# Convolution taps of chunk 0 as products with diagonal matrices, in a fused attention and gated feed-forward kernel

## The chip, the cores and the metric

The kernel runs on one core of one Trainium2 chip. That core has a matrix engine (TensorE, PE in the profile, its weight loads PEld), a vector engine (VectorE, DVE), an activation engine (ScalarE, ACT), a general engine (GpSimd, POOL) and a queue engine (SyncE, SP). The metric is the device time of one execution in microseconds, and lower is better.

## What is computed

```python
# attention, for batch 4, 8 heads, 768 rows, head size 64
k_sum = k.reshape(B, H, nb, 32, D).max(axis=3)      # one key per block of 32
v_sum = v.reshape(B, H, nb, 32, D).mean(axis=3)
scores_l = scale * q @ k.T      # kept where |row - column| < 16
scores_s = scale * q @ k_sum.T + log(32)
a = softmax(concat([masked scores_l, scores_s]))
x = a @ concat([v, v_sum])      # heads side by side: (4, 768, 512)
# feed-forward
h = maximum(x @ w_in, 0)        # (4, 768, 1024)
conv_out = sum over k in 0..2 of conv_w[k] * (h shifted by k - 1 rows)
gate = 1 / (1 + exp(-conv_out))
out = (h * gate) @ w_out
```

Everything is float32.

## The kernel before

A sequence of 768 rows is cut in two chunks of 384 rows, so four batches make eight chunks, numbered 0 to 7. Within a chunk attention runs over four pairs of heads. The feed-forward part is worked on transposed: the 1024 hidden features lie on partitions in eight blocks (`fc` 0 to 7), the rows along the free dimension. One block of one chunk is a unit.

The large products with `w_in` and `w_out` are done in three reduced-precision terms each: a number is split into a high and a low part (`win_hi`, `win_lo`, `xh`, `xl`, `ghi`, `glo`, `wout_hi`, `wout_lo`), and high by high, high by low and low by high are added up in PSUM. The weights come in as 64-bit words and are decoded and split on the core (`decode`, `weights`: lines 97 to 104 on ACT and DVE, 127 on ACT, 128 on POOL). Scores (line 260), weighted values (line 329) and transposes (line 308) are products of plain float32.

A unit goes like this. `f1` (line 404) does 12 matmuls of 384 or 386 columns into a PSUM tile with the tag `f1`, of which there are three buffers. `gate_conv` rectifies the tile in place on ACT (line 422), makes the middle tap of the convolution in a new SBUF tile `t` (line 425 on ACT for the chunks in `TAP_ACT`, line 427 on DVE for the others), and adds the outer two taps on DVE (line 434), reading the PSUM tile at shifted columns. `gate_mul` takes the tanh on ACT (line 451), multiplies on DVE with the rectified rows (line 452), rounds to `ghi` on ACT (line 455) and makes `glo` on POOL (line 456). `gate_mul` runs one unit later than `gate_conv`; the PSUM tile is free after line 452. `f2` (line 473) contracts the gated rows with `w_out`, in pieces spread over the units of the next chunks, and line 482 with a DMA on ACT's queue stores the result.

Chunk 0 starts with the attention of its own rows alone (the loop at line 507), while the inputs arrive in the order of `LOADS` on SP's queue. The convolution weights are the item `c` of that list (line 504), and are decoded after the loop (line 518). Units 0 and 1 of chunk 0 do three quarters of their first product early (line 521). The weights `w_out` are split from unit 6 of chunk 0 on (`OUT_AT`). `WARM` adds idle matmuls (line 78) in chunk 0, three behind each unit's first product.

The order of the instructions on each engine is made by a planner from the program's order and its own idea of their lengths. From chunk 2 on (`ORDERED`), the order of the matrix engine is that of the program. On each engine the instructions run in that fixed order, and a wait holds up what stands behind it.

Of the kernel before, what the change touches and what calls it, by code (L numbers as in the profile page):

```python
# [7 lines left out]
F32 = mybir.dt.float32  # L8
F32R = mybir.dt.float32r
U32 = mybir.dt.uint32  # L10
AF = mybir.ActivationFunctionType
ALU = mybir.AluOpType
# [3 lines left out]
DM, DF = 512, 1024  # L16
P = 128
# [9 lines left out]
CH = S // 2  # L27
CB = CH // QB
NCC = DM // P
NFC = DF // P  # L30
# [3 lines left out]
DEPTH = 2  # L34


TAP_ACT = (0, 1, 2, 4)


LOADS = "k0 q0 k1 q1 v0 k2 q2 a0 v1 k3 q3 a1 w0 v2 c a2 w1 v3 a3 w2 w3 w4 w5 w6 w7"  # L40
EARLY_IN = 2

OUT_AT = (6, 7, 8, 9, 10, 10, 11, 12)
# [7 lines left out]
def attention_ffn(ctx, tc, qT, kT, vT, v4, w_in, cwT, w_out, mask8, ident_in, out):  # L51
    nc = tc.nc
    cp = ctx.enter_context(tc.tile_pool(name="cp", bufs=1))
    sp = ctx.enter_context(tc.tile_pool(name="sp", bufs=2))
    ps = ctx.enter_context(tc.tile_pool(name="ps", bufs=1, space=bass.MemoryType.PSUM))
# [3 lines left out]
    ident = cp.tile([P, P], F32, name="ident")  # L59
    cw = cp.tile([P, NFC, 3], F32, name="cw")  # L60
    win_hi = cp.tile([P, NFC, NCC, P], F32R, name="win_hi")
    win_lo = cp.tile([P, NFC, NCC, P], F32R, name="win_lo")
    wout_hi = cp.tile([P, NFC, DM], F32R, name="wout_hi")
    wout_lo = cp.tile([P, NFC, DM], F32R, name="wout_lo")

    raw_a = cp.tile([P, 6, 1024], U32, name="raw_a", tag="big_a")
    raw_b = cp.tile([P, 6, 1024], U32, name="raw_b", tag="big_b")
# [21 lines left out]
    def decode(out, words, n, name):  # L89

        lo_word = words[:, 0 : 2 * n : 2]
        hi_word = words[:, 1 : 2 * n : 2]
        low = sp.tile([P, DM], U32, tag="wl", name=f"wl_{name}", bufs=1)[:, :n]
        nc.scalar.activation(
            out.bitcast(F32), hi_word.bitcast(F32), AF.Abs, scale=2.0**-112
        )
        nc.vector.tensor_scalar(low, lo_word, 29, None, ALU.logical_shift_right)  # L100
        nc.vector.scalar_tensor_tensor(
            out, out, 3, low, ALU.logical_shift_left, ALU.bitwise_or
        )
        nc.vector.scalar_tensor_tensor(
            out, hi_word, 0x80000000, out, ALU.bitwise_and, ALU.bitwise_or
        )
# [12 lines left out]
        return t  # L119

    def split_out(fc, t):
        weights(t, wout_hi[:, fc, :], wout_lo[:, fc, :], f"o{fc}")

    def weights(words, hi, lo, name):
        w = sp.tile([P, DM], U32, tag="wu", name=f"wu_{name}", bufs=3)
        decode(w, words, DM, name)
        nc.scalar.copy(hi, w.bitcast(F32))  # L127
        nc.gpsimd.tensor_tensor(lo, w.bitcast(F32), hi.bitcast(F32), ALU.subtract)  # L128
# [8 lines left out]
    for tag in ("xh", "xl"):  # L137
        t = sp.tile([P, 2, KL], F32, tag=tag, name=f"k_{tag}", bufs=2)
# [11 lines left out]
    def load_k(c, p):  # L150
        b, hf = divmod(c, 2)
        i = c * NP + p
        st = state[(c, p)] = {}
        if i == NP - 1:
            kw = sp.tile([P, 1024], F32, tag="stage", name=f"kw{i}", bufs=2)
            st["kw"] = kw[:, : CB * NK].rearrange("p (b k) -> p b k", b=CB)
        else:
            st["kw"] = sp.tile([P, CB, NK], F32, tag="kw", name=f"kw{i}", bufs=3)
        if hf == 0:
            if c == 0:  # L160
                k = spare[p]
            else:
                k = sp.tile([P, KL], F32, tag="kT", name=f"kT{i}", bufs=2)
            nc.sync.dma_start(k, kT[b, p, :, :KL])
            st["k"] = k
        if c:
            first = kT[b, p, :, hf * CH : hf * CH + WK]
            nc.sync.dma_start(st["kw"][:, :, :WK], window(first, 1, [SP, P], WK))

    def load_vt(c, p):  # L170
        b, hf = divmod(c, 2)
        i = c * NP + p
        if hf:
            return
        if b == 0:
            v = raw_b[:, 2 + p, :S].bitcast(F32)
        else:
            v = sp.tile([P, 1024], F32, tag="stage", name=f"vt{i}", bufs=2)[:, :S]
        nc.sync.dma_start(v, vT[b, p])
        state[(c, p)]["vt"] = v  # L180
# [15 lines left out]
    def load_vm(c, p):  # L196
        vm = state[("vm", c // 2, p)]
        nc.sync.dma_start(
            state[(c, p)]["va"][WK:NK, :, :], vm.unsqueeze(1).to_broadcast([NB, CB, P])
        )  # L200
# [158 lines left out]
    def slot(j):  # L359

        if j % 2 == 0:
            n = j // 2 + 2
            if NP <= n < npair:
                load_k(*divmod(n, NP))
                load_vt(*divmod(n, NP))
            if NP <= j // 2 < npair:
                load_vm(*divmod(j // 2, NP))
            if j // 2 < npair:
                qk(*divmod(j // 2, NP))
        else:  # L370
            n = (j + 1) // 2
            if NP <= n + 1 < npair:
                load_q(*divmod(n + 1, NP))
            if n < npair:
                c, p = divmod(n, NP)
                if c:
                    vmean_pair(c, p)
                    load_v(c, p)
                prep_pair(c, p)
# [32 lines left out]

    held = {}

    def gate_conv(c, fc):


        hf = c % 2
        n = CH + 2 * hf
        ng = CH - 1 + 2 * hf  # L420
        h = f1ps.pop((c, fc))
        nc.scalar.activation(h[:, :n], h[:, :n], AF.Relu)
        t = sp.tile([P, CH + 2], F32, tag="t", name=f"t{c}_{fc}", bufs=3)[:, :ng]
        if c in TAP_ACT:
            nc.scalar.activation(t, h[:, hf : hf + ng], AF.Copy, scale=cw[:, fc, 1:2])  # L425
        else:
            nc.vector.tensor_scalar(
                t, h[:, hf : hf + ng], cw[:, fc, 1:2], 1.0, ALU.mult, ALU.mult
            )
        for k in (0, 2):  # L430

            i0 = max(0, 1 - hf - k)
            i1 = min(ng, n - (hf + k - 1))
            nc.vector.scalar_tensor_tensor(  # L434
                t[:, i0:i1],
                h[:, hf + k - 1 + i0 : hf + k - 1 + i1],
                cw[:, fc, k : k + 1],
                t[:, i0:i1],
                ALU.mult,
                ALU.add,  # L440
            )
        held[(c, fc)] = h, t

    def gate_mul(c, fc):

        hf = c % 2
        ng = CH - 1 + 2 * hf
        d0 = (CH - 1) * hf
        h, t = held.pop((c, fc))
        hi = gated["hi"][:, fc, d0 : d0 + ng]  # L450
        nc.scalar.activation(t, t, AF.Tanh, scale=0.5)  # L451
        nc.vector.scalar_tensor_tensor(  # L452
            t, t, 1.0, h[:, hf : hf + ng], ALU.add, ALU.mult
        )
        nc.scalar.copy(hi, t)  # L455
        nc.gpsimd.tensor_tensor(  # L456
            gated["lo"][:, fc, d0 : d0 + ng], t, hi.bitcast(F32), ALU.subtract
        )
# [3 lines left out]
    def f2(b, st, fcs, tag="f2", bufs=1):  # L462
        if fcs[0] == 0:
            f2ps[(b, st)] = ps.tile([P, 512], F32, tag=tag, name=f"f2_{b}_{st}", bufs=bufs)
        po = f2ps[(b, st)]
        ss = slice(st * P, (st + 1) * P)
        ghi, glo = gated["hi"], gated["lo"]
        for fc in fcs:
            contracted.add((b, st, fc))
            for m, (gx, w) in enumerate(  # L470
                ((ghi, wout_hi), (ghi, wout_lo), (glo, wout_hi))
            ):
                nc.tensor.matmul(  # L473
                    po,
                    gx[:, fc, ss],
                    w[:, fc, :],
                    start=(fc == 0 and m == 0),
                    stop=(fc == NFC - 1 and m == 2),
                )
        if fcs[-1] == NFC - 1:  # L480
            ob = sp.tile([P, DM], F32, tag="wu", name=f"ob{b}_{st}", bufs=3)
            nc.scalar.activation(ob, po, AF.Copy, scale=0.5)  # L482
            nc.scalar.dma_start(out[b, ss, :], ob)
# [3 lines left out]
    cw_words = sp.tile([P, 2 * NFC * 3], U32, tag="cww", name="cw_words", bufs=1)  # L487
    nc.scalar.dma_start(mask, mask8)
    nc.scalar.dma_start(ident, ident_in)

    for item in LOADS.split():
        what, n = item[0], int(item[1:] or 0)
        if what == "k":
            load_k(0, n)
        elif what == "q":
            load_q(0, n)
        elif what == "v":
            load_vt(0, n)
        elif what == "a":
            load_v(0, n)  # L500
        elif what == "w":
            raws[n] = load_in(n)
        else:
            nc.sync.dma_start(cw_words, cwT.bitcast(U32))

    prep_pair(0, 0)
    for j in range(2 * NP):
        slot(j)
        if j % 2 == 0:
            vmean_pair(0, j // 2)  # L510
        slot_t(j)
        slot_av(j)
# [2 lines left out]
            slot_t(j)  # L515
        slot_av(j)

    decode(cw.rearrange("p f k -> p (f k)").bitcast(U32), cw_words, NFC * 3, "cw")
    for fc in range(EARLY_IN):
        split_in(fc, raws[fc])  # L520
    for cc in range(3):
# [158 lines left out]
```

## Time and profile before

| what | value |
|---|---|
| median of 3 timed runs | 409.43 us (408.94, 409.43, 410.58) |
| span of the profiled execution, first to last instruction | 408.4 us |
| instructions | 8852 |
| mean granted clock of the matrix engine | 0.986 |
| first and last rectification of a unit (line 422), start | 41.2 us, 380.1 us |
| first products of chunk 0's unit 2 begin | 59.09 us |

The profile has the span alone for its execution; the median stands 1.0 us above that span. Busy time counts an engine's running instructions, not its waits; matmuls overlap, so a busy matrix engine is not one at its peak. The granted clock is the share of full speed that the matrix engine's throttle let through. Where a timeline row ends in brackets, they hold the idle time before it and what ended it.

### The profile page before, as it was taken

How to read it: one execution, taken by the hardware profiler on the slowest of the kernel's cores; microseconds unless marked ns; L12 is line 12 of the kernel's file. 1: busy time of each engine (PE TensorE's matmuls, PEld its weight loads, DVE VectorE, ACT ScalarE, POOL GpSimd, SP SyncE). 2: the span in 40 equal slices, each digit the busy share in tenths (PEclk: the TensorE clock that was granted, in tenths of full speed). 3: DMA queues.
4: the chain of work that ended last, by engine and by line, in shares of the span. 5: the costliest groups of instructions: out<-in, count | busy, mean ns of one | idle time of the engine just before them, and what ended most of it. 6: DMA issues, size and time to landing. Idle time of an engine off the chain costs nothing.

```text
span 408.4 us, 8852 instructions
## 1 busy us (share of the span) xinstructions
PE 385.8 (94%) x3173; PEld 319.2 (78%) x3173; DVE 269.9 (66%) x809; ACT 251.8 (62%) x774; POOL 150.7 (37%) x179
## 2 busy tenths in 40 slices
PE   7989669997799999999999999999999999999996
PEld 3546458785678888888888888888788888898884
DVE  4999888999956765768775466556566665566200
ACT  3664887997867676757566777666564654343211
POOL 2226564477754233333333333333332232112100
PEclk9999989999969999999999999999999999999999
DMA  8999943767865784456344344344220000000011
GB/s 290 331 367 202 258 138 114 227 185 223 225 145 170 240 285 126 127 154 181 85 111 112 78 112 112 77 120 119 66 63 27 28 0 27 26 27 26 27 51 51
DMA packets 60715, 54.47 MB, mean 133 GB/s; under 512 B 24640, under 2 KB 51328, under 8 KB 60672
## 3 DMA queue, kind: packets, MB, share of 16 engines
q1 hardware_dynamic: 56928, 47.19, 41.4%
q10 hardware_dynamic: 3744, 6.73, 4.6%
q8 instruction: 25, 0.41, 0.4%
q14 instruction: 18, 0.15, 0.1%
HBM read 45.55 MB, written 6.29 MB: 127 GB/s over the span
## 4 chain that ended last, share of the span: by engine, by line
PE 62%; ACT 14%; DVE 13%; POOL 5%; issue 4%; DMA 1%; SPq 0%; ACTq 0%; POOLq 0%; DVEq 0%
PE f L473 26%; PE f L404 23%; ACT a L288 6%; PE pt L308 4%; PE xp L329 4%; PE pq L260 4%; DVE t L434 4%; ACT t L451 2%; PE pw L78 2%; POOL glo L456 2%; DVE t L452 1%; POOL a L300 1%; DMA k_xh<-kT 1%; ACT ghi L455 1%; POOL wout_lo L128 1%
## 5 line engine op out<-in xcount | busy, mean ns | idle before, releaser
L456 POOL TENSOR_TENSOR glo<-t,ghi 128x383 fp32r<-128x383 f32 (+1 forms) x64 | 66.8, 1044 | 128.5 <-ACT ghi L455 124.4
L404 PE MATMUL f<-xh,win_hi 128*128 128x384 f32 (+1 forms) x256 | 93.4, 365 | 0.9 <-ACT win_hi L127 0.9
L434 DVE SCALAR_TENSOR_TENSOR t<-f,cw,t 128x382 f32<-128x382 f32 (+3 forms) x128 | 78.7, 615 | 20.7 <-ACT t L425 17.8
L404 PE MATMUL f<-xl,win_hi 128*128 128x384 f32 (+1 forms) x256 | 87.8, 343 | 0.0
L404 PE MATMUL f<-xh,win_lo 128*128 128x384 f32 (+1 forms) x256 | 87.3, 341 | 0.0
L288 ACT ACTIVATE a<-a,nm 128x120 f32<-128x120 f32 x192 | 73.1, 382 | 9.9 <-DVE nm L278 9.7
L473 PE MATMUL f<-wout_lo,ghi 128*128 128x512 f32 x192 | 76.0, 396 | 2.4 <-POOL wout_lo L128 2.4
L473 PE MATMUL f<-wout_hi,ghi 128*128 128x512 f32 x192 | 76.2, 397 | 0.0
L473 PE MATMUL f<-wout_hi,glo 128*128 128x512 f32 x192 | 75.3, 393 | 0.0
L451 ACT ACTIVATE t<-t 128x383 f32<-128x383 f32 (+1 forms) x64 | 33.6, 525 | 63.8 <-DVE t L434 63.2
L300 POOL TENSOR_TENSOR a<-a,sm 128x360 f32<-128x360 f32 x56 | 45.4, 832 | 55.2 <-DVE sm L297 51.4
L452 DVE SCALAR_TENSOR_TENSOR t<-t,f 128x383 f32<-128x383 f32 (+1 forms) x64 | 35.3, 552 | 26.6 <-ACT t L451 26.6
L404 PEld LDWEIGHTS f<-xh,win_hi 128*128 128x128 f32 x256 | 49.1, 192 | 3.6 <-ACT win_hi L127 1.2
L404 PEld LDWEIGHTS f<-xl,win_hi 128*128 128x128 f32 x256 | 49.2, 192 | 0.7 <-issue 0.2
L404 PEld LDWEIGHTS f<-xh,win_lo 128*128 128x128 f32 x256 | 48.9, 191 | 0.2
L473 PEld LDWEIGHTS f<-wout_lo,ghi 128*128 128x128 f32 x192 | 36.2, 189 | 8.9 <-POOL wout_lo L128 3.0
L455 ACT CAST ghi<-t 128x383 fp32r<-128x383 f32 (+1 forms) x64 | 32.5, 508 | 16.4 <-DVE t L452 15.6
L278 DVE CUSTOM_DVE_ANT_0 a<-pq,mask 128x120 f32<-128x120 f32 x192 | 42.2, 275 | 0.0
L473 PEld LDWEIGHTS f<-wout_hi,glo 128*128 128x128 f32 x192 | 36.2, 188 | 7.7
L308 PE MATMUL pt<-ident,a 128*120 128x128 f32 x192 | 34.4, 285 | 7.8 <-ACT aT L315 3.6
L473 PEld LDWEIGHTS f<-wout_hi,ghi 128*128 128x128 f32 x192 | 36.3, 189 | 6.4 <-ACT ob L482 0.3
L260 PEld LDWEIGHTS pq<-kw,q 64*64 64x64 f32 x768 | 23.3, 133 | 20.8 <-issue 12.8
(59 smaller groups left out, 506.7 us busy)
## 6 DMA issues: line engine op xcount, KB each, us to landing
va<-v SPq DMA_DIRECT2D x32, 288.0 KB
kw<-kT SPq DMA_DIRECT2D x28, 288.0 KB
q<-qT SPq DMA_DIRECT2D x32, 192.0 KB
out_dram<-ob ACTq DMA_DIRECT2D x24, 256.0 KB
kT<-kT SPq DMA_DIRECT2D x12, 392.0 KB
vt<-vT SPq DMA_DIRECT2D x12, 384.0 KB
wo<-w_out SPq DMA_DIRECT2D x8, 512.0 KB
raw_a<-w_in SPq DMA_DIRECT2D x6, 512.0 KB
```

The lines of the kernel that those rows point to most:

```text
L260: last = nc.tensor.matmul(pq[h][half * QB : (half + 1) * QB, i * NK : (i + 1) * NK], st["q"][r, blk * QB : (blk + 1) * QB], st["kw"][r, bl ...
L278: nc.vector.tensor_tensor_reduce(a[:, i, :], pq[h][:, i * NK : (i + 1) * NK], mask[:, hf, i, :], -0.125, 3.0e38, ALU.add, ALU.min, nm[:, h ...
L288: nc.scalar.activation(a[:, i, :], a[:, i, :], AF.Exp, bias=nm[:, h, i : i + 1], scale=-1.0, accum_out=sm[:, h, i : i + 1],)
L300: (nc.gpsimd if n >= NP else nc.vector).tensor_tensor(a, a, sm[:, h, :].unsqueeze(2).to_broadcast([P, 3, NK]), ALU.mult)
L308: last = nc.tensor.transpose(pt[:NK, i * P : (i + 1) * P], a[:, i, :], ident)
L404: last = nc.tensor.matmul(ph[:, :n], w[:, fc, cc, :], x[:, cc, :n], start=(cc == 0 and m == 0), stop=(cc == NCC - 1 and m == 2),)
L434: nc.vector.scalar_tensor_tensor(t[:, i0:i1], h[:, hf + k - 1 + i0 : hf + k - 1 + i1], cw[:, fc, k : k + 1], t[:, i0:i1], ALU.mult, ALU.add,)
L451: nc.scalar.activation(t, t, AF.Tanh, scale=0.5)
L452: nc.vector.scalar_tensor_tensor(t, t, 1.0, h[:, hf : hf + ng], ALU.add, ALU.mult)
L455: nc.scalar.copy(hi, t)
L456: nc.gpsimd.tensor_tensor(gated["lo"][:, fc, d0 : d0 + ng], t, hi.bitcast(F32), ALU.subtract)
L473: nc.tensor.matmul(po, gx[:, fc, ss], w[:, fc, :], start=(fc == 0 and m == 0), stop=(fc == NFC - 1 and m == 2),)
```

## The change

For chunk 0 alone (`TAP_PE`), the three taps become three float32 products on the matrix engine. The stationary operand of tap `k` is a diagonal matrix that holds the 128 weights of the block; the moving operand are the rectified rows, shifted by `k - 1` columns, and the three add up in a PSUM tile of the tag `f1`. For that the rows are rectified out of PSUM into an SBUF tile (`rows`), the tanh works in place on the PSUM tile, and line 452's product goes from both to an SBUF tile `t`.

The diagonals (128 x 384 for the three taps of a block) are made by POOL in eight operations, one in each turn of the first attention loop, from the identity matrix and the decoded weights. So the convolution weights are loaded earlier, on ACT's queue, and decoded after the first turn. Rows and diagonals have the memory of `wout_hi` and `wout_lo`, which become one tile for each block. The list of chunks whose middle tap ACT makes goes from 0, 1, 2, 4 to 1, 2, 3, 5.

```diff
-TAP_ACT = (0, 1, 2, 4)
+TAP_ACT = (1, 2, 3, 5)
+TAP_PE = (0,)
-LOADS = "k0 q0 k1 q1 v0 k2 q2 a0 v1 k3 q3 a1 w0 v2 c a2 w1 v3 a3 w2 w3 w4 w5 w6 w7"
+LOADS = "k0 q0 k1 q1 v0 k2 q2 a0 v1 k3 q3 a1 w0 v2 a2 w1 v3 a3 w2 w3 w4 w5 w6 w7"
...
-    wout_hi = cp.tile([P, NFC, DM], F32R, name="wout_hi")
-    wout_lo = cp.tile([P, NFC, DM], F32R, name="wout_lo")
+    wout_hi, wout_lo = {}, {}
+    rows = [cp.tile([P, DM], F32, name=f"row{fc}", tag=f"wh{fc}") for fc in range(NFC)]
+    diag = [cp.tile([P, DM], F32, name=f"diag{fc}", tag=f"wl{fc}") for fc in range(NFC)]
...
     def split_out(fc, t):
-        weights(t, wout_hi[:, fc, :], wout_lo[:, fc, :], f"o{fc}")
+        wout_hi[fc] = cp.tile([P, DM], F32R, name=f"wout_hi{fc}", tag=f"wh{fc}")
+        wout_lo[fc] = cp.tile([P, DM], F32R, name=f"wout_lo{fc}", tag=f"wl{fc}")
+        weights(t, wout_hi[fc], wout_lo[fc], f"o{fc}")
...
+    def taps(fc):
+        return diag[fc][:, : 3 * P].rearrange("p (k i) -> p k i", k=3)
+
+    def diagonal(fc):
+        nc.gpsimd.tensor_tensor(
+            taps(fc),
+            ident.unsqueeze(1).to_broadcast([P, 3, P]),
+            cw[:, fc, :].unsqueeze(2).to_broadcast([P, 3, P]),
+            ALU.mult,
+        )
...
         h = f1ps.pop((c, fc))
+        if c in TAP_PE:
+            row = rows[fc][:, :n]
+            nc.scalar.activation(row, h[:, :n], AF.Relu)
+            conv = ps.tile([P, 512], F32, tag="f1", name=f"cv{c}_{fc}", bufs=3)
+            for k in (1, 0, 2):
+                i0 = max(0, 1 - hf - k)
+                i1 = min(ng, n - (hf + k - 1))
+                nc.tensor.matmul(
+                    conv[:, i0:i1],
+                    taps(fc)[:, k, :],
+                    row[:, hf + k - 1 + i0 : hf + k - 1 + i1],
+                    start=k == 1,
+                    stop=k == 2,
+                )
+            held[(c, fc)] = row, conv[:, :ng]
+            return
...
-        nc.scalar.activation(t, t, AF.Tanh, scale=0.5)
+        th = t
+        nc.scalar.activation(th, th, AF.Tanh, scale=0.5)
+        if c in TAP_PE:
+            t = sp.tile([P, CH + 2], F32, tag="t", name=f"t{c}_{fc}", bufs=3)[:, :ng]
         nc.vector.scalar_tensor_tensor(
-            t, t, 1.0, h[:, hf : hf + ng], ALU.add, ALU.mult
+            t, th, 1.0, h[:, hf : hf + ng], ALU.add, ALU.mult
         )
...
     nc.scalar.dma_start(ident, ident_in)
+    nc.scalar.dma_start(cw_words, cwT.bitcast(U32))
...
         slot(j)
+        if j == 0:
+            decode(cw.rearrange("p f k -> p (f k)").bitcast(U32), cw_words, NFC * 3, "cw")
+        diagonal(j)
         if j % 2 == 0:
             vmean_pair(0, j // 2)
...
-    decode(cw.rearrange("p f k -> p (f k)").bitcast(U32), cw_words, NFC * 3, "cw")
     for fc in range(EARLY_IN):
         split_in(fc, raws[fc])
```

More of the change, by code (lines that the diff above doesn't have):

```diff
@@ L475, in f2 @@
                     gx[:, fc, ss],
-                    w[:, fc, :],
+                    w[fc],
                     start=(fc == 0 and m == 0),
@@ L500, in attention_ffn @@
             load_v(0, n)
-        elif what == "w":
+        else:
             raws[n] = load_in(n)
-        else:
-            nc.sync.dma_start(cw_words, cwT.bitcast(U32))
     prep_pair(0, 0)
```

## The prediction

> **What bounds the kernel now.** I read the page first, then busy time by stage, then the matrix engine's timeline inside the stages where it isn't full, then the chain of work that ended last.
>
> ```profile
> PE 385.8 (94%) x3173; PEld 319.2 (78%) x3173; DVE 269.9 (66%) x809; ACT 251.8 (62%) x774; POOL 150.7 (37%) x179
> ...
> 41.00:59.00 18.00, 11.18 (x152) 8.27 (x152) 14.62 (x62) 15.20 (x57) 11.10 (x11) 1.00 0.83 222
> 59.00:63.00 4.00, 4.00 (x18) 3.64 (x15) 4.00 (x15) 3.38 (x15) 1.62 (x2) 0.59 0.01 2
> 63.00:92.00 29.00, 28.88 (x273) 23.14 (x271) 26.12 (x78) 25.26 (x80) 15.34 (x20) 1.00 0.63 187
> 92.00:113.00 21.00, 15.86 (x139) 12.26 (x139) 20.46 (x55) 16.17 (x43) 16.10 (x16) 1.00 0.81 224
> 113.00:121.00 8.00, 8.00 (x44) 5.83 (x43) 5.12 (x10) 5.59 (x18) 5.09 (x5) 0.57 0.74 165
> 121.00:384.00 263.00, 261.70 (x2133) 228.86 (x2133) 165.00 (x492) 161.22 (x487) 85.62 (x106) 1.00 0.34 97
> 384.00:408.40 24.40, 20.74 (x91) 16.81 (x90) 0.00 (x0) 2.90 (x5) 1.02 (x1) 0.97 0.14 54
> ```
>
> The columns after a window's length are busy time of PE, PEld, DVE, ACT and POOL, then the granted clock. From 121 to 384 us PE lacks 1.3 us of 263. Whatever delays PE before 121 us therefore delays the end one for one, and what DVE or ACT save after 121 saves nothing. Chunk 0's gates lie between 41 and 92 us. There PE is full from 63 to 92 (28.88 of 29), and it is slack in four places: 6.82 us idle between 41 and 59, 5.14 us idle between 92 and 113, and two stretches at a low clock, worth 4 x 0.41 = 1.64 us and 8 x 0.43 = 3.44 us. In all 17.0 us. DVE is nearly full where PE idles (20.46 of 21).
>
> ```profile
> 47.40 0.54 PE L308 MATMUL pt<-ident,a 128*120 128x128 f32 x3 [1.42 <-POOL a L300]
> 52.61 0.54 PE L308 MATMUL pt<-ident,a 128*120 128x128 f32 x3 [1.69 <-POOL a L300]
> 57.71 0.52 PE L308 MATMUL pt<-ident,a 128*120 128x128 f32 x3 [2.08 <-ACT aT L315]
> 59.90 0.52 PE L404 MATMUL f<-xh,win_lo 128*128 128x384 f32 x1
> 60.22 0.52 PE L404 MATMUL f<-xh,win_hi 128*128 128x384 f32 x1
> ...
> 63.91 0.34 PE L404 MATMUL f<-xh,win_hi 128*128 128x384 f32 x1
> 64.08 0.34 PE L404 MATMUL f<-xl,win_hi 128*128 128x384 f32 x1
> ...
> 93.72 0.85 PE L260 MATMUL pq<-kw,q 64*64 64x120 f32 x24 [1.70 <-POOL kw L217]
> 112.44 0.50 PE L473 MATMUL f<-wout_lo,ghi 128*128 128x512 f32 x1 [1.87 <-POOL wout_lo L128]
> ```
>
> The holes end on softmax rows, on an ACT copy, on a key copy and on an output weight. After the holes the first products start 0.32 us apart (59.90 to 60.22), when warm 0.17 (63.91 to 64.08).
>
> The chain tells the same: it runs on PE from 59.16, leaves it at 77.50, and comes back to stay at 112.44.
>
> ```profile
> 59.16 3.72 PE f L404 x12
> ...
> 77.50 0.48 ACT aT L315
> ...
> 110.71 1.69 POOL wout_lo L128
> ...
> 112.44 0.74 PE f L473 x2
> ```
>
> So the question is whether new PE work in chunk 0 fits into 17.0 us of slack, and how much of the slack the relief of DVE and ACT really opens.
>
> **What is added on PE.** Eight units times three taps are 24 float32 products, 128 x 128 against 383 columns. The trace has float32 products only in small tiles:
>
> ```profile
> L260 PE MATMUL pq<-kw,q x768: 262/263/459, 6.4 to 323.2; 64*64 64x120 f32 x192
> ...
> L329 PE MATMUL xp<-aT,va x768: 222/222/370, 17.8 to 344.1; 120*64 120x64 f32 x192
> ```
>
> Both lines issue 12 products per head pair (six blocks, two heads), 384 over 32 pairs, yet each has 768 records: a float32 product is two matmuls. From 64 to 120 columns a record grows by 41 ns, 0.73 ns a column. The split products advance 0.17 us per 384 columns, 0.45 ns a column. So a float32 record streams at more than half as much again, most simply at half rate. Estimates for one record of 383 columns: by the slope 0.28 us, by twice the split pitch 0.35. I take 0.32, so 0.64 a tap, 1.92 a unit, and 48 x 0.32 = 15.4 us in all. Bounds: 48 x 0.175 = 8.4 us if a record costs what a split one does, and 48 x 0.455 = 21.8 if records don't overlap (222 ns and 0.73 for each of 319 further columns).
>
> The Trainium skill, Perfetto Trace Analysis, section Engine Utilization, halves the output rate for the type it calls FP32_LOW_HIGH. Read as the price of a whole product, that is a sum of about 8 us; read per record it is my 15.4. No run here shows a full-size float32 product.
>
> **What is removed.** In chunk 0, 16 DVE taps and 8 ACT taps go:
>
> ```profile
> L434 DVE SCALAR_TENSOR_TENSOR t<-f,cw,t 128x382 f32<-128x382 f32 x32 | 19.6, 614 | 15.6 <-ACT t L425 15.2
> ...
> L425 ACT ACTIVATE t<-f,cw 128x383 f32<-128x383 f32 x24 | 13.9, 578 | 0.9
> ```
>
> That is 16 x 0.61 = 9.8 us of DVE and 8 x 0.58 = 4.6 us of ACT. Neither is on the path while PE is full (59 to 92). They count only through PE's holes. Rectifying into SBUF instead of in place, the tanh in PSUM and the product of both have the same shapes as now: nothing, with a tenth of a microsecond either way per unit as bounds.
>
> **What the slack gives back.**
>
> ```profile
> 53.56 0.49 ACT L422 ACTIVATE f<-f 128x384 f32<-128x384 f32 x1
> ...
> L422 ACT ACTIVATE f<-f x64: 463/475/497, 41.2 to 380.1; 128x384 f32<-128x384 f32 x32, 128x386 f32<-128x386 f32 x32
> ```
>
> (1) Units 0 and 1 are rectified at 41.2 and 53.56, so their six tap products (3.84 us) become ready among the holes of 41 to 59. I take 3.0 of them as hidden; ends 0 and 3.84. (2) With PE busier there, the low clock from 59 to 63 should mostly not occur: 1.2 of 1.64, ends 0 and 1.64. (3) From 92 to 113 PE waits because DVE, ACT and POOL are behind after 30 us at about 90% load. In the new kernel PE's chunk 0 is some 11 us longer (six units of 1.92) and the others have 14 us less to do, so they arrive level: 4.0 of 5.14 goes, ends 0 and 5.14. What is late next is DVE itself, whose chunk-1 taps and weight decoding don't shrink. (4) The low clock behind the last hole: 2.5 of 3.44, ends 0 and 3.44. Together 10.7 us, ends 0 and 14.1.
>
> **The new waits.** Each unit's taps stand on PE behind ACT's rectification, with the next attention and first products queued behind them. Three filler matmuls lie between, 0.66 us in the first row, which cover a prompt ACT, not a late one:
>
> ```profile
> 62.88 0.66 PE pw L78 x3
> ...
> 62.55 0.33 PE L404 MATMUL f<-xh,win_lo 128*128 128x384 f32 x1
> 62.92 0.47 ACT L422 ACTIVATE f<-f 128x384 f32<-128x384 f32 x1 [0.61 <-PE f L404]
> ...
> 78.18 0.33 PE L404 MATMUL f<-xh,win_lo 128*128 128x384 f32 x1
> ...
> 81.67 0.47 ACT L422 ACTIVATE f<-f 128x384 f32<-128x384 f32 x1
> ```
>
> Once ACT follows at once, once 3.2 us late, behind the exponentials. The planner that orders this chunk will put other work between, where it foresees that. The three PSUM buffers now hold two tiles a unit: a unit's first product waits for the gate product (tanh on ACT, then DVE) of two units before, not of three. I take 2.0 us for both, a quarter microsecond a unit; ends 0 and 10 (eight times 1.2).
>
> **The early part.** Eight diagonals on POOL in the first 30 us, and the tap weights' load and decode moved ahead:
>
> ```profile
> L300 POOL TENSOR_TENSOR a<-a,sm 128x360 f32<-128x360 f32 x56 | 45.4, 832 | 55.2 <-DVE sm L297 51.4 <-ACT wu_o L97 2.9 <-DVE nm L278 0.9
> ...
> 5.00:30.00 25.00, 7.07 (x12) 1.00 1.06 353
> ...
> 9.95 0.33 SPq L504 DMA_DIRECT2D cw_words<-cwT  x1
> ...
> 7.96 0.39 ACT L288 ACTIVATE a<-a,nm 128x120 f32<-128x120 f32 x1 [5.01 <-DVE nm L278]
> ...
> 12.32 0.96 DVE L300 TENSOR_TENSOR a<-a,sm 128x360 f32<-128x360 f32 x2
> ...
> 20.14 1.60 DVE L300 TENSOR_TENSOR a<-a,sm 128x360 f32<-128x360 f32 x2
> 20.47 0.89 POOL L238 COPY va<-vm 24x768 f32<-24x768 f32 x1 [4.30 <-ACT vm L236]
> ```
>
> The nearest operation gives 0.83 x 384/360 = 0.89 us each, 7.1 in all, on a POOL that is busy 7.07 of 25 us. Behind a diagonal wait the key and value copies, for which PE's scores wait; beside POOL the DVE pair took 1.60 instead of 0.96. Ends: 0, and 8 x 0.64 = 5.1 us. I take 0.5, since POOL has room and the diagonals aren't needed before 41 us. The load is one issue of 0.33 us that leaves SP's queue, whose later loads move up by that, and becomes ACT's third. ACT computes nothing before 7.96 us, so nothing is behind it but the table load. The decode is the same four small operations, now nearer the start, and its cost lies inside the 0.5.
>
> The **ACT tap on chunks 1, 2, 3, 5** instead of 0, 1, 2, 4: chunks 3 and 5 trade eight DVE taps for ACT ones, chunk 4 the reverse. All lie past 121 us under a full PE, with DVE at 165 and ACT at 161 of 263: nothing. Uncovered, a chunk's trade is 8 x 0.6 = 5 us.
>
> **The sum.** 15.4 - 3.0 - 1.2 - 4.0 - 2.5 + 2.0 + 0.5 = +7.2 us on the span of 408.4, so 415.6. The median of the runs shown, 409.43, lies 1.0 above that span, so I forecast 416.6.
>
> **The rivals.** *(B) PE waits for ACT.* Units wait 0.8 us on average (6.4 in all) and only 6.2 of the slack returns: 15.4 - 6.2 + 6.4 + 0.5 = +16.1, 425.5. For it: the 3.2 us lag. Against: ACT has 4.6 us less to do. *(C) PE is filled.* All 14.1 us return, no new wait, half a microsecond of early cost: +1.8, and DVE's four earliest taps, gone before 59 us, pull PE forward by up to 2: 409.4 to 411. For it: PE ran 63 to 92 without a hole beside DVE at 90%. Against: the holes before 59 come from softmax and weight decoding, which stay. *(D) DVE decides, faster.* If the stretch from 41 to 121 is paced by DVE, the 9.8 us taken from it let all 17.0 us close and pull the 59 us start forward by four taps' 4 x 0.61 = 2.4: 15.4 - 17.0 - 2.4 = -4.0, 405.4. To be faster by 2 us, 17.4 us must come back, more than all the slack without the pull. Against: PE alone is full from 59 to 92, where most taps sit. *(E) A float32 product costs half.* 8.4 - 10.7 + 2.5 = +0.2, 409.6. That is the reading of the Trainium skill's rate named above. Against: the slope of 0.73 ns. *(F) It doesn't do what it says* (the planner leaves the taps in a lump): a form of B, not priced by itself.
>
> **How the numbers follow.** Forecast 0.55 (own range 411.5 to 421), B 0.22, C 0.12, D 0.06, E 0.05. A measurement of this kernel can tell about 0.5% (2 us) from no change: faster is below 407.4, slower above 411.5. Faster: D and part of E, 0.08. Same: C and the rest of E, 0.15. Slower: 0.77. The range 409.5 to 426 leaves out D and half of B, and E just stays inside.
>
> **What would show it.** Forty-eight records of 383 columns on PE, 0.32 us apart (E if 0.17). PE idle between 41 and 59 down to about 4 us. Chunk 1's part of the timeline with under 2 us of holes and no low clock. Waits of PE on the rectification totalling about 2 us (B if over 6). DVE busy about 10 us less. What would make it wrong: a product at other than 0.64 us, or a planner's order that lets ACT's lag onto PE.

## The result, and the profile after

The changed kernel takes 421.54 us in the median of 4 runs (420.35 to 423.54), against 409.25 us for the kernel before beside it: a ratio of 1.0295, 95% interval 1.0246 to 1.0344. That is 12.3 us more. 416.6 was forecast, with a range of 409.5 to 426: the direction and the range hold, the size was too small by 5 us. The profiled execution has a span of 419.6 us, 11.2 more than before.

First the page's line of busy times, then busy time by stage, with the columns as above (idle time is a window's length less PE's busy time).

```profile
PE 400.2 (95%) x3221; PEld 325.9 (78%) x3221; DVE 259.9 (62%) x785; ACT 252.8 (60%) x774; POOL 156.1 (37%) x187
...
0.00:30.00 30.00, 22.17 (x210) 11.50 (x211) 22.96 (x80) 13.87 (x54) 16.74 (x25) 1.00 0.99 297
30.00:41.00 11.00, 9.85 (x87) 6.66 (x87) 10.51 (x19) 7.02 (x19) 3.44 (x4) 1.00 0.92 268
41.00:59.00 18.00, 15.90 (x119) 9.49 (x118) 14.00 (x55) 12.68 (x47) 11.12 (x10) 0.81 0.74 191
59.00:92.00 33.00, 32.85 (x256) 22.46 (x256) 18.55 (x52) 18.54 (x58) 14.96 (x19) 1.00 0.58 170
92.00:120.00 28.00, 27.25 (x252) 22.09 (x244) 24.58 (x73) 23.82 (x75) 15.13 (x17) 1.00 0.80 234
120.00:130.00 10.00, 8.27 (x77) 6.31 (x76) 9.97 (x25) 6.70 (x22) 5.62 (x6) 0.92 0.75 220
130.00:395.00 265.00, 262.96 (x2152) 230.41 (x2150) 159.21 (x485) 167.32 (x500) 88.06 (x108) 1.00 0.32 89
```

The first two stages of the kernel before, for comparison:

```profile
0.00:30.00 30.00, 25.62 (x247) 13.46 (x248) 23.85 (x88) 16.63 (x64) 7.27 (x16) 1.00 0.99 329
30.00:41.00 11.00, 9.86 (x88) 7.00 (x87) 10.71 (x16) 5.46 (x10) 7.53 (x6) 1.00 1.00 212
```

DVE has 10.0 us less to do than before, as forecast, but between 59 and 92 it is now busy only 18.55 of 33 us while PE is full (32.85). Much of the relief was given where PE did not wait. From 92 to 120 PE idles 0.75 us and the clock is full; from 120 to 130 it idles 1.73 us at a clock of 0.92. Before, the stretch from 92 to 113 alone had 5.14 us of holes and a low clock behind them. Up to 41 us PE idles 9.0 us, for 5.5 before, and from 41 to 59 it idles 2.1, for 6.8.

The tap products themselves, by their line:

```profile
L444 PEld LDWEIGHTS cv<-row,diag x48: 186/190/192, 53.8 to 98.0; 128*128 128x128 f32 x48
L444 PE MATMUL cv<-row,diag x48: 484/485/589, 53.8 to 98.3; 128*128 128x383 f32 x32, 128*128 128x382 f32 x16
...
53.83 2.19 PE L444 MATMUL cv<-row,diag 128*128 128x383 f32 x6
55.96 0.42 PE L264 MATMUL pq<-kw,q 64*64 64x120 f32 x4
```

There are 48 records of 485 ns that overlap. In the timeline the unit that begins at 53.83 hands over to the next work at 55.96, so six records take 2.13 us, 0.355 each: twice the 0.175 of a split product. Eight units make 17.0 us.

The same milestones in both traces show where the time went: the end of the first attention stage (its last weighted values), and the rectifications of chunk 0's unit 0 and of the first unit of chunks 1 and 2. The kernel before comes first, then the changed one.

```profile
32.30 0.91 PE L329 MATMUL xp<-aT,va 120*64 120x64 f32 x22
...
41.24 0.47 ACT L422 ACTIVATE f<-f 128x384 f32<-128x384 f32 x1
...
84.42 0.47 ACT L422 ACTIVATE f<-f 128x386 f32<-128x386 f32 x1
```

```profile
38.19 0.91 PE L333 MATMUL xp<-aT,va 120*64 120x64 f32 x22
...
52.74 0.49 ACT L439 ACTIVATE row<-f 128x384 f32<-128x384 f32 x1
...
102.42 0.47 ACT L453 ACTIVATE f<-f 128x386 f32<-128x386 f32 x1
```

| milestone | before, us | after, us | later by |
|---|---|---|---|
| first stage's last weighted values begin | 32.30 | 38.19 | 5.9 |
| chunk 0, unit 0 rectified | 41.24 | 52.74 | 11.5 |
| chunk 0, unit 2 rectified | 57.46 | 62.28 | 4.8 |
| chunk 0, unit 7 rectified | 81.67 | 96.08 | 14.4 |
| chunk 1, first unit rectified | 84.42 | 102.42 | 18.0 |
| chunk 2, first unit rectified | 135.33 | 145.67 | 10.3 |
| last unit rectified | 380.14 | 391.37 | 11.2 |

Counting the rectifications also corrects the table ahead of the prediction: the products that begin at 59.09 us before are unit 3's, not unit 2's, since unit 2 is rectified at 57.46.

By the start of chunk 1 the delay is 18.0 us, as much as the whole 17.0 us of tap products and one more. Chunk 1 gives 7.7 us back. Behind it the two traces run alike to 0.9 us. PE's order also differs between the two kernels, so such a difference is the sum of several effects.

### The profile page after: what moved, and what is told of

It reads as the page before. It is cut to its first block, busy times and chain, and to the rows that moved or that the text cites. A ratio compares the mean times of both kernels' runs of the same rounds, so it can differ in the third digit from the quotient of the medians.

```text
span 419.6 us, 8954 instructions
## 1 busy us (share of the span) xinstructions
PE 400.2 (95%) x3221; PEld 325.9 (78%) x3221; DVE 259.9 (62%) x785; ACT 252.8 (60%) x774; POOL 156.1 (37%) x187
## 4 chain that ended last, share of the span: by engine, by line
PE 55%; ACT 18%; DVE 14%; DMA 8%; issue 3%; POOL 1%; SPq 0%; ACTq 0%; DVEq 0%; POOLq 0%
PE f L507 22%; PE f L408 19%; ACT a L292 8%; DVE t L465 6%; DMA raw_b<-vT 5%; PE cv L444 4%; PE pq L264 3%; PE xp L333 3%; PE pt L312 3%; DVE t L486 2%; ACT t L483 2%; ACT t L456 2%; ACT ghi L489 2%; PE pw L80 2%; DVE wu_o L103 1%
## 5 line engine op out<-in xcount | busy, mean ns | idle before, releaser
L490 POOL TENSOR_TENSOR glo<-t,ghi 128x383 fp32r<-128x383 f32 (+1 forms) x64 | 65.8, 1028 | 127.6 <-ACT ghi L489 117.3
L465 DVE SCALAR_TENSOR_TENSOR t<-f,cw,t 128x385 f32<-128x385 f32 (+1 forms) x112 | 69.1, 617 | 31.6 <-ACT t L456 29.1
L483 ACT ACTIVATE t<-t 128x385 f32<-128x385 f32 (+1 forms) x56 | 29.4, 525 | 66.1 <-DVE t L465 66.0
L486 DVE SCALAR_TENSOR_TENSOR t<-t,f 128x385 f32<-128x385 f32 (+1 forms) x56 | 30.9, 554 | 25.8 <-ACT t L483 25.8
L264 PEld LDWEIGHTS pq<-kw,q 64*64 64x64 f32 x768 | 22.2, 135 | 18.7 <-issue 12.8
```

The source lines that it names most:

```text
L264: last = nc.tensor.matmul(pq[h][half * QB : (half + 1) * QB, i * NK : (i + 1) * NK], st["q"][r, blk * QB : (blk + 1) * QB], st["kw"][r, bl ...
L465: nc.vector.scalar_tensor_tensor(t[:, i0:i1], h[:, hf + k - 1 + i0 : hf + k - 1 + i1], cw[:, fc, k : k + 1], t[:, i0:i1], ALU.mult, ALU.add,)
L483: nc.scalar.activation(th, th, AF.Tanh, scale=0.5)
L486: nc.vector.scalar_tensor_tensor(t, th, 1.0, h[:, hf : hf + ng], ALU.add, ALU.mult)
L490: nc.gpsimd.tensor_tensor(gated["lo"][:, fc, d0 : d0 + ng], t, hi.bitcast(F32), ALU.subtract)
```

## The experiments

The kernel before took longer in the later groups of runs (medians of 409.3, 412.7, 411.8 and 412.8 us in the four groups), so runs are compared by their ratio to the kernel before of their own group.

| run | median, us | ratio to before | 95% interval |
|---|---|---|---|
| changed kernel, second time | 422.77 | 1.0248 | 1.0170 to 1.0326 |
| diagonals later in the program (e9) | 418.52 | 1.0159 | 1.0097 to 1.0221 |
| middle tap alone (e3) | 414.11 | 1.0058 | 1.0021 to 1.0095 |
| before, no fillers (e6) | 410.48 | 0.9997 | 0.9960 to 1.0035 |
| load, decode and diagonals later in the program (e2) | 421.26 | 1.0192 | 1.0120 to 1.0264 |
| taps in the reduced type (e7) | 413.39 | 1.0030 | 0.9992 to 1.0067 |
| changed, no fillers (e5) | 417.63 | 1.0111 | 1.0045 to 1.0176 |
| before, load and decode early (e1) | 405.54 | 0.9813 | 0.9743 to 0.9883 |
| the same, second time | 406.23 | 0.9862 | 0.9810 to 0.9914 |
| before, load alone moved (e10) | 403.92 | 0.9826 | 0.9760 to 0.9892 |
| taps of two units on PE (e8) | 412.74 | 1.0020 | 0.9985 to 1.0055 |
| before, ACT taps moved (e4) | 412.12 | 0.9996 | 0.9956 to 1.0036 |

The changed kernel ran a second time beside others:

> The changed kernel once more, beside the others of this call, since the kernel before took 412.7 us in the last call and 409.3 in the first. No theory is tested; its ratio to the kernel before should be 1.02 to 1.035.

Its ratio lies inside the first interval (1.0248, in 1.0246 to 1.0344), and its median of 422.77 is the partner of the runs beside it.

### Is PE's time the price?

Two runs shorten the tap products and leave the waits, the tiles and the early part in place. The first leaves out the outer taps:

```diff
-            for k in (1, 0, 2):
+            for k in (1,):
```

> The changed kernel with the middle tap alone on PE; the outer two taps are left out. 32 of 48 matmuls go, 32 x 0.353 = 11.3 us of PE; all waits, tiles and the early part stay. Theory (PE time is the price and is paid almost in full in chunk 0): 8 to 11 us less than the changed kernel, close to the run with the reduced type. Rival (the waits are the price): 3 us less or nothing.

The second makes rows and diagonals in the split products' type, and every tap reads all 384 columns unshifted:

```diff
-rows = [cp.tile([P, DM], F32, ...
-diag = [cp.tile([P, DM], F32, ...
+rows = [cp.tile([P, DM], F32R, ...
+diag = [cp.tile([P, DM], F32R, ...
...
-                    row[:, hf + k - 1 + i0 : hf + k - 1 + i1],
+                    row,
```

> The changed kernel with the tap products in the reduced type of the split products: 24 matmuls instead of 48, some 0.18 us each instead of 0.35; the shift of the outer taps and full precision are left out, all waits, tiles and the early part stay. Theory (PE time is the price): 17.0 - 4.2 = 12.8 us less PE work; DVE, ACT and POOL then bound chunk 1 again, so not all of it returns: 409 to 413 us. Rival (the new waits of PE on ACT and on the PSUM tiles, or the early part, are the price): 417 or more.

With 11.3 us of PE work left out, e3 is 8.7 us faster than the changed kernel in its group (414.11 to 422.77). With 12.8 us left out, e7 comes from 1.0248 and 1.0295 to 1.0030, which is 9 to 11 us; its 413.39 us lie just above the 409 to 413 that were expected, in a group where the kernel before took 412.7. Some 70 to 85% of the PE time comes back, with every wait in place. In e7's trace the 24 records have the length of a split product (337 ns in the kernel before):

```profile
L444 PE MATMUL cv<-row,diag x24: 334/339/446, 53.6 to 88.1; 128*128 128x384 f32 x24
```

The rival, that waits are the main price, falls. The changed kernel's trace says the same. Of the waits of PE's weight loads, these end on the rectified rows (us in total, times, longest):

```profile
PEld cv L444 <- ACT row L439: 1.2, 5, 0.4
```

### Is PE time in chunk 0 worth the same before and after?

The three filler matmuls behind each unit's first product in chunk 0 leave, 24 x 0.216 = 5.2 us, once in each kernel:

```diff
-WARM = {"start": 10, ..., "av": 3, "unit": 3}
+WARM = {"start": 10, ..., "av": 3}
```

> The changed kernel without the three filler matmuls behind each unit's first product in chunk 0 (24 matmuls, 24 x 0.216 = 5.2 us of PE). Theory (PE binds through chunk 0 in the changed kernel): 3 to 5 us less, 416.5 to 418.5. Rival (the tap products wait for ACT, and the fillers only cover that wait): within 1 us of 421.5, with waits of PE in place of the fillers.

> The kernel before without the three filler matmuls behind each unit's first product in chunk 0 (5.2 us of PE). Theory (before, PE is full from 59 to 92 us but the next stretch waits for DVE, ACT and POOL anyway, so PE time saved in chunk 0 comes back as holes): 0 to 2 us less than the kernel before, with more holes between 85 and 113 us, where the changed kernel gained 4 from the same edit. Rival (PE time in chunk 0 is worth its full price before, too): 4 to 5 us less.

The changed kernel gains 5.1 us by the medians (417.63 to 422.77, in two groups; the intervals of the ratios 1.0111 and 1.0248 just touch), the kernel before nothing (0.9997). The stages of the kernel before without fillers:

```profile
59.00:92.00 33.00, 31.39 (x295) 26.67 (x295) 29.69 (x92) 29.23 (x96) 16.32 (x22) 0.95 0.52 150
92.00:113.00 21.00, 17.19 (x149) 13.20 (x150) 18.38 (x40) 14.85 (x41) 12.90 (x14) 0.92 0.68 197
```

And those of the changed kernel without fillers:

```profile
59.00:92.00 33.00, 32.33 (x264) 23.37 (x260) 20.38 (x65) 20.80 (x69) 14.72 (x18) 1.00 0.52 157
92.00:113.00 21.00, 19.87 (x207) 16.63 (x203) 16.47 (x52) 17.83 (x56) 11.73 (x14) 1.00 0.76 220
```

In the first, unit 7 is rectified 3.5 us sooner (78.15 for 81.67), but chunk 2 starts at 135.01, for 135.33. From unit 2's rectification to there PE is busy 4.2 us less, and its holes grow from 5.5 to 8.1 us, so 2.6 of the 4.2 come back as holes. Another 1.3 us are lost ahead of it: unit 2 is rectified at 58.72, for 57.46, and the clock from 41 to 59 is 0.81, for 1.00. In the changed kernel the holes of the same stretch hardly grow (3.3 us, for 3.0 in its second trace), and chunk 2 starts 4.4 us sooner (142.59 for 147.01).

DVE is at 29.69 of 33 us in the first and at 20.38 in the second. But in the first the holes from 59 to 135 end mostly on output weights made by POOL (4.2 us) and on an ACT copy (2.5), so which engine paces the work there is not shown. Nor is the edit pure dummy work: from 41 to 59 the clock is lower without the fillers in both kernels (0.81 for 1.00, and 0.72 for 0.81), and that part was not separated. What the two answers show is that the change makes PE the bound of a stretch in which PE had waited for other engines too.

### What does the early part cost?

The diagonals move behind the first stage, two before chunk 0's units and then one a unit:

```diff
-        diagonal(j)
...
     for fc in range(EARLY_IN):
         split_in(fc, raws[fc])
+    for fc in range(EARLY_IN):
+        diagonal(fc)
...
+        if c == 0 and u + EARLY_IN < NFC:
+            diagonal(u + EARLY_IN)
```

> The changed kernel with the convolution weights loaded and decoded early, as it has them, but the diagonals made late (two before chunk 0's units, then one a unit). Theory A (the early diagonals slow the first stage, and that reaches the end): 2 to 4 us less than the changed kernel. Theory B (the first stage is hidden in PE's holes before 59 us, and what the diagonals cost there they cost elsewhere): within 2 us of the changed kernel.

e9 runs in 418.44 to 419.04, the changed kernel beside it in 421.04 to 423.11: 4.2 us less by the medians, just above the 2 to 4 of theory A. But the trace shows that this run doesn't test theory A. The planner still puts all eight diagonals into the first stage, one at 10.38 and seven in a row up to 26.28, where the changed kernel has them in five pieces from 10.49 to 25.0:

```profile
10.38 0.83 POOL L423 TENSOR_TENSOR diag<-ident,cw 128x384 f32<-128x384 f32 x1 [1.11 <-DVE cw L106]
...
19.84 6.44 POOL L423 TENSOR_TENSOR diag<-ident,cw 128x384 f32<-128x384 f32 x7
```

So the gain belongs to another planned order. The first stage's last weighted values come at 36.42, for 38.19 and 39.32 in the changed kernel's two traces. Of that lead little or nothing is left when unit 2 is rectified (62.32, for 62.28 and 63.43), and most of the gain appears behind it: chunk 2 starts at 143.28, for 145.67 and 147.01. What the eight diagonals cost is therefore not shown. In the changed kernel they take 0.82 to 1.12 us each, and beside them DVE's pair of normalizations takes 1.85, where it took 0.96 before:

```profile
L423 POOL TENSOR_TENSOR diag<-ident,cw x8: 822/911/1115, 10.5 to 24.2; 128x384 f32<-128x384 f32 x8
...
12.59 1.85 DVE L304 TENSOR_TENSOR a<-a,sm 128x360 f32<-128x360 f32 x2
```

Moving the load and the decode back as well adds, to e9's edit, the item `c` in `LOADS` and the decode behind the loop:

> The changed kernel with the load and the decode of the convolution weights where the kernel before has them, and the diagonals made late, two before chunk 0's units and then one a unit. Theory (the 17 us of PE time for the taps carry the loss, the slow first stage is mostly hidden in PE's holes before 59 us): 418 to 421 us, first stage back at about 33 us. Rival (the early part carries a large share of the 12 us): 415 or less.

At 1.0192 it isn't separated from the changed kernel (1.0248 and 1.0295). Its 421.26 us lie at the upper end of the 418 to 421 that were expected, and the rival, 415 or less, falls. Its first stage ends no sooner than e9's (36.62), so the part of the expectation that put it back at 33 us failed, although load and decode are back in their places. Here too the planner makes the diagonals ahead of the units, from 27.6 to 41.4 us, among the weight splitting on POOL (9.46 of 11 us busy from 30 to 41). Neither run has the diagonals out of the way of the first stage, so this question stays open.

The load alone was tried on the kernel before, first with the early decode and then without (the item `c` leaves `LOADS`, and in the first two runs the decode leaves its place behind the loop):

```diff
     nc.scalar.dma_start(ident, ident_in)
+    nc.scalar.dma_start(cw_words, cwT.bitcast(U32))
...
+        if j == 0:
+            decode(cw..., cw_words, NFC * 3, "cw")
```

> The kernel before with one part of the change alone: the convolution weights are loaded on ACT's queue as its third transfer and decoded after the first turn; taps stay on ACT and DVE, no diagonals. Theory: in the changed kernel SP's third key load was issued at 4.93 us behind the mask's landing, instead of 3.08, so this move alone delays the first attention stage; the weighted values of chunk 0 end some 2 to 4 us later than in the kernel before (33.1 us), and the holes of PE between 41 and 59 us take up part of it: 0 to +3 us on the time. Rival (the prediction's reading: the load costs nothing): the first stage ends within 0.5 us of before, time within 1 us.

> The kernel before with the convolution weights loaded on ACT's queue and decoded early, once more: it took 405.5 us, 0.981 of the kernel before, where 0 to +3 us was expected. Theory (the gain is real and comes from another planned order, in which PE's holes in chunk 1 are spread and no low clock follows them): ratio 0.975 to 0.99, no low clock between 90 and 130 us. Rival (a chance of that run): ratio above 0.993.

> The kernel before with the convolution weights loaded on ACT's queue as its third transfer, but decoded where it decodes them now, behind the attention loop. Theory (the move of the transfer shifts every load of the first stage behind another landing, and only the other planned order of the early decode gains): 0 to +3 us against the kernel before. Rival (the move of the transfer itself gains): 3 us or more less, like the run with both.

Both expectations of a cost failed, and the rival of the third run, that the move itself gains, held: the load on ACT's queue makes the kernel before faster, by 1.4 to 1.9%. The repeat came out as expected (0.9862). With the load alone (e10) the lowest median of the study is reached, 403.92 us. The mechanism that was expected is there, and doesn't decide: in e10 SP's third key load is issued at 5.02 us, for 3.08 before, and the first stage's last weighted values begin at 34.39 (34.93 and 36.02 in the two runs with the decode), for 32.30. The gain comes in chunk 1, which takes 45.9 us from its first rectification to chunk 2's (45.5 in both runs with the decode), for 50.9 before. The stages of e10:

```profile
59.00:92.00 33.00, 32.77 (x308) 26.21 (x310) 31.83 (x94) 30.73 (x98) 20.38 (x25) 1.00 0.64 185
92.00:113.00 21.00, 17.67 (x147) 13.12 (x145) 19.76 (x51) 16.80 (x50) 13.69 (x12) 1.00 0.92 230
113.00:121.00 8.00, 7.49 (x72) 6.16 (x67) 5.64 (x22) 6.36 (x20) 4.80 (x5) 1.00 0.80 206
```

Before, the holes from 92 to 113 were 5.14 us and the next 8 us ran at a clock of 0.57. Here they are 3.33 us and the clock stays at 1.00. The planner also gives PE another order in this kernel. It isn't a run's luck with the clock: at a mean granted clock of 0.99 or more the kernel before took 408.6 to 411.2 us in this group, and e10 403.7 to 404.0. Whether the order, the arrival of loads or the clock that follows the holes makes the gain was not separated. With the taps on PE the gain isn't seen: e9, with the early load and decode, and e2, without them, stand at 1.0159 and 1.0192, inside each other's intervals.

### Are tap products free where PE had holes?

e9's kernel, with taps on PE for units 0 and 1 of chunk 0 alone, the others as before, and the diagonals of these two units alone (they run at 10.2 and 19.7 us):

```diff
-TAP_ACT = (1, 2, 3, 5)
+TAP_ACT = (0, 1, 2, 4)
...
-        if c in TAP_PE:
+        if c in TAP_PE and fc < EARLY_IN:
```

> The kernel before with the early load and decode, and the taps of chunk 0's units 0 and 1 alone as products on PE (12 matmuls of 0.353 us, 4.2 us of PE, in the stretch where PE had 6.8 us of holes); diagonals late, the middle tap on ACT for chunks 0, 1, 2, 4. Theory (PE work is free where PE has holes): within 2 us of the run with the early load alone, perhaps 1 us less. Rival (PE work costs its price anywhere before 121 us): 3 to 4 us more than that run.

The ratio is 1.0020, for 0.9862 of the run with the early load in the same group: 6.5 us lost for 4.2 us of PE work, more than either side expected. Unit 2 is rectified at 61.02, against 57.24 and 58.45 in the two runs of the early load:

```profile
61.02 0.47 ACT L453 ACTIVATE f<-f 128x384 f32<-128x384 f32 x1 [0.16 <-PE f L408]
```

```profile
57.24 0.49 ACT L422 ACTIVATE f<-f 128x384 f32<-128x384 f32 x1
```

```profile
58.45 0.48 ACT L422 ACTIVATE f<-f 128x384 f32<-128x384 f32 x1
```

So 2.6 to 3.8 of the 4.2 us are paid by then, although the first stage ends about as it does there (35.12, for 34.93 and 36.02) and PE has the holes: from 41 to 59 it still idles 3.7 us, for 5.6 and 5.8, at a clock of 0.81, for 0.94 and 1.00. Four of unit 0's six records run at the low clock, a pair of them in 1.65 us instead of the 0.81 of the pair at 40.40. The products weren't free beside the holes. Unit 7 is rectified 0.5 to 1.8 us later, and chunk 2 starts 6.3 to 7.7 us later, so more is lost in chunk 1, with a hole of 2.4 us and one of 1.0 on the output weights:

```profile
112.82 0.50 PE L507 MATMUL f<-wout_lo,ghi 128*128 128x512 f32 x1 [2.40 <-POOL wout_lo L132]
...
124.53 0.50 PE L507 MATMUL f<-wout_lo,ghi 128*128 128x512 f32 x1 [1.03 <-POOL wout_lo L132]
```

This kernel has another planned order too, so that the products alone make the delay is not shown.

### The ACT taps behind 121 us

```diff
-TAP_ACT = (0, 1, 2, 4)
+TAP_ACT = (0, 1, 2, 3, 5)
```

> The kernel before with the middle tap on ACT for chunks 0, 1, 2, 3, 5 instead of 0, 1, 2, 4: the part of the change that lies behind 121 us. Theory (PE is full there, so it costs nothing): within 1 us of the kernel before. Rival (DVE or ACT paces some of these chunks): 2 us or more either way.

The ratio is 0.9996, within 0.4% either way, with the same order of instructions on PE. Whether ACT or DVE makes the middle tap of chunks 3 to 5, behind 121 us, doesn't matter, as forecast.

## Why the prediction was right, and where it was off

The sign and the range came out, and for the main reason forecast: PE time in chunk 0 that the slack doesn't give back. The size was 5 us low, and the terms were not all right.

- **What bounds the kernel.** Right. PE is full behind chunk 1 in both traces, and what was lost before it reached the end: 10.3 us at chunk 2's start, 11.2 at the last rectification. e4 confirms that the choice of the middle tap's engine behind 121 us doesn't count.
- **The price of a product.** The step was right, two records at half rate, and the size low: 0.355 us for 0.32, 17.0 us for 15.4. Twice the split pitch was the better of the two estimates. The reading of the Trainium skill's rate (Perfetto Trace Analysis, Engine Utilization) as a whole product's price, rival E, falls: about 8 us by it, 17.0 measured. Read for each of two records it is nearer, 15.4.
- **Credits (1) and (2), the holes before 59 us and the low clock behind them, 4.2 us.** This step failed: none of it is seen. When unit 2 is rectified the changed kernel is 4.8 us late, and the tap products of units 0 and 1 are 4.3. The holes between 41 and 59 did close (2.10 us of idle, for 6.82), but 3.5 us of others opened before 41, and the clock from 41 to 59 was lower (0.81, for 1.00). The credit took unit 0 as rectified at 41.2; in the changed kernel it was rectified at 52.74, behind the holes, so its taps weren't ready for them. The first stage was 5.9 us late, but that alone isn't the cause: in e8 it ends as early as without taps, unit 0 is rectified at 39.07, and unit 2 still comes 2.6 to 3.8 us later. Why the holes don't take the products stays open; the planned order differs in each of these kernels.
- **The early part, 0.5 us.** Not settled. The first stage ended 5.9 us later, where the prediction had almost nothing. The moved load makes 2.1 of that by itself (e10), at no loss of time; what the diagonals add wasn't isolated, since the planner left them in the first stage in e9 and e2. What the moved load does was read the wrong way: with the rest as before it gains 1.4 to 1.9%.
- **Credits (3) and (4), chunk 1's holes and low clock, 6.5 us.** The direction was right: chunk 1 is 7.7 us shorter (43.3 us between the milestones, for 50.9). The reason is shown in part only. The holes in it shrink from 5.1 to 2.4 us, 2.7 of the 4.0 booked, and by the mean granted clock (0.96, for 0.93) the low clock costs an estimated 1.7 us, for 3.6, 1.8 of the 2.5 booked; the rest is not accounted for. e10 and the runs with the early decode shorten chunk 1 by 5.1 to 5.4 us with DVE's taps where they were, so the relief of DVE needn't be what does it.
- **The new waits, 2.0 us.** 1.2 us on the rectified rows; ACT was late at times, and the planner had put attention work in between. Rival B's waits of 6.4 us didn't occur. The measured 12.3 us still lie nearer to its 16.1 than to the 7.2 forecast, because little of the slack came back; B had put that at 6.2 us.
- **The sum by the traces:** 17.0 of products, 1.0 more by chunk 1's start for all that the early part and the holes left over, -7.7 in chunk 1, +0.9 behind it: 11.2, which is the difference of the two spans. The forecast had 15.4 - 4.2 - 6.5 + 2.0 + 0.5 = 7.2.
- **Rivals C and D** needed most or all of the slack back. By the start of chunk 2 the delay is 10.3 us, so 6.7 of the 17.0 us of products are made up for.

## What to carry to other kernels

Work that moves to the fullest engine is paid at the price of that stage, whatever it frees elsewhere. Idle time of that engine in the stages beside it counts only if the work is ready there, and here it mostly wasn't given back even beside holes. To see whether an engine binds a stage, take a few microseconds of dummy work off it: here the same edit was worth 5 us in one kernel and nothing in the other. An edit of the program is not yet an edit of the order: where a planner or compiler orders the work, look in the trace where the moved work runs before reading the time. Two runs here were meant to make the diagonals late, and both still made them ahead of chunk 0's units.

## What was not expected of the hardware

**The clock of one program differs from run to run.** The kernel with the early load was profiled twice. Each time PE had a hole of 2.61 us, up to 57.49 us in the first and 58.71 in the second, and then the same products in the same order. The windows from 60 to 64 us, of the first and of the second profile:

```profile
60.00:64.00 4.00, 3.93 (x12) 3.59 (x14) 2.56 (x7) 1.71 (x9) 0.46 (x1) 0.53 0.10 15
```

```profile
60.00:64.00 4.00, 3.91 (x25) 3.25 (x23) 3.77 (x11) 4.00 (x16) 1.25 (x2) 1.00 0.02 6
```

The granted clock is 0.53 in one and 1.00 in the other. So low clock such as the 1.64 and 3.44 us that the prediction counted as slack of the kernel before can come or not come behind the same hole. The Trainium skill, TensorE: Matmul & The Clock Gate, section What's actually happening, says that the gate watches a free-running window; these two runs agree with that, but don't prove it.

**A small load on another queue delays the next loads.** The changed kernel's third key load, and the load of the same keys before, on SP's queue:

```profile
4.93 0.33 SPq L168 DMA_DIRECT2D k_xl<-kT  x1
```

```profile
3.08 0.43 SPq L164 DMA_DIRECT2D k_xl<-kT  x1
```

SP's waits in the changed kernel (us in total, times, longest) name what it waited for at that line:

```profile
SPq L168 <- DMA mask<-mask: 1.8, 1, 1.8
...
SPq L168 <- DMA cw_words<-cwT: 0.8, 1, 0.8
```

A key load needs neither the mask nor the tap words. With the load's move as the only edit (e10) the same key load is issued at 5.02 us, so the move is enough to delay it; why it then waits for these landings no trace here shows. That the move made the kernel before faster was not foreseen, and its cause is open.
